# Weight pieces of the first stage converted in turn, and one attention half moved to earlier iterations

## The chip, the core and the metric

The kernel runs on one core of a Trainium2 chip. The metric is the time of one execution on the device in microseconds (us), as the median of several runs. The engines are TensorE (PE in the profile; its weight loads are PEld), VectorE (DVE), ScalarE (ACT), GpSimd (POOL) and SyncE (SP), which issues most DMA transfers. Each engine takes its instructions strictly in its own order. An instruction waits until what it needs is there, and all that stands behind it on that engine waits with it.

## What is computed

```python
p_packed = sm_attn(p, k, v)          # 8 batches, 8 heads, 576 keys, 32 packed rows, 64 wide
out = sm_attn(q, p_packed, p_packed) # second attention, over the 32 packed rows
x = out.transpose(0, 2, 1, 3).reshape(4608, 512)
h = x @ w_in                         # 512 x 2048, arrives as 64-bit floats
x = (h - tanh(h)) @ w_out            # 2048 x 512, arrives as 64-bit floats
# then a layer of 8 experts: every token goes to the expert of its largest gate
```

## The kernel before

**Stages.** The first stage computes the packed rows, the first attention, for 12 of 16 *units* (a unit is four heads of one batch); the other four units are done later. It also converts 24 of 32 weight pieces. The second stage goes over 16 half batches: each time 16 steps of a first layer (`up`, with tanh) and a second layer (`down`). The third stage runs the experts. Only the first stage is changed.

**One iteration `u` of the first stage** (14 of them) does for different units at once: k of unit u+1 is transposed on PE (`k_up`, line 318) and copied out by ACT (line 321, tile `kT`, one buffer); the exponential of unit u runs on ACT (`expo_b`, line 340); the weights of unit u-1 are turned (`e_up`: on DVE at line 351 for the units up to 7, on PE at line 358 with copies on ACT, line 362, and DVE, line 360, from unit 8 on); unit u-2 is multiplied with v on PE (`pack`, lines 371 and 373) and copied out by ACT (line 374, from a single buffer `po`); then the scores of unit u+1 are taken on PE (line 330), and DVE reduces them to a maximum (`expo`, line 334, tile `mx`).

**Weight pieces.** `plan` is the list of pieces, each 128 x 512 numbers of 64 bits: 16 of `w_in`, 16 of `w_out`. Piece i is loaded by SP (lines 202 and 170) into one of five buffers, when the piece that had it has been read; it is narrowed to 32 bits by ACT (line 125), POOL (line 126) and two passes on DVE (lines 131 and 133). That is all for `w_in`. A piece of `w_out` is then also split into a rounded part (ACT, line 184) and a rest (DVE, line 188), at the start of the next iteration ("late"). POOL writes a piece of `w_out` in place, so it comes after ACT; and its buffer is free only after line 133, that of `w_in` after line 131. Iteration u converts pieces 2u and 2u+1.

**Jobs.** The table `jobs` says which piece of side work an iteration appends after `expo`: `make_z` turns packed rows (DVE, line 216); `att_q`, `att_s`, `att_f`, `att_x`, `att_n`, `att_t`, `att_l` are the steps of the second attention for the first half of batch 0 (`att_s` on PE; `att_x` on DVE, lines 249 and 250, then ACT, line 252; `att_t` ends in `a_hi`, `att_l` in `a_lo` on DVE, line 270); `fuse` multiplies the packed rows with a quarter of `w_in` on PE (line 277), and `fuse_h` (ACT, line 281) and `fuse_l` (DVE, line 285) split this product into `wf_hi` and `wf_lo`. The first `up` of the second stage (lines 603 to 605) needs `a_hi`, `a_lo`, `wf_hi` and `wf_lo`; the first `down` (lines 629 to 631) accumulates in four banks, one of which was `po`.

Inside a stage each engine keeps the order of the code. Between the end of the first stage and the start of the second, the order on an engine is decided when the kernel is built, by what is expected to be ready first.

```python
for u in range(LA):                              # LA = 14, UA = 12
    ...                                          # share, k_up, e_up, expo_b
    for n in late: part_h(n)                     # w_out pieces of the iteration before
    for n in late: part_l(n)
    ...                                          # ACT and POOL part of the next pieces
    if 1 < u < UA + 2: pack(u - 2)
    if u + 1 < UA: score(u + 1); expo(u + 1)
    ...                                          # loads of k, v, pieces, p, q
    for fn in jobs.get(u, ()): fn()
    for x in range(done, due(u)): convert(x)     # pieces 2u, 2u+1
```

Of the kernel before, what the change touches and what calls it, by code (L numbers as in the profile page):

```python
# [27 lines left out]
NF = DFF // 128  # L28
# [10 lines left out]
HF = NF // 2  # L39
# [11 lines left out]
def attention_moe_kernel(ctx: ExitStack, tc: tile.TileContext, q, k, v, p, w_in, w_out, w_gate, w_og, w1, w2, out):  # L51
# [130 lines left out]
    def part_h(f):  # L182
        sv, hi, _ = part_of(f)
        act.activation(hi, sv, AF.Copy)
# [23 lines left out]
    def make_z(b, hs=range(4)):  # L208
        if b not in z_t:
            z_t[b] = ef.tile([128, 4, 32], F32, name="zt", bufs=2)  # L210
        z = z_t[b]
        for g in range(2):
            for h in hs:
                for e in range(2):
                    r = 64 * (h % 2) + 32 * e
                    vec.transpose(z[r:r + 32, 2 * g + h // 2], pp[32 * h:32 * h + 32, 2 * b + g, 32 * e:32 * e + 32])
# [3 lines left out]
    def load_q(b, hf, js=range(4)):  # L220
        if (b, hf) not in q_t:
            q_t[b, hf] = tmp["new"]("qt", [128, 4, HB, 32])
        qt = q_t[b, hf]
        src = q[b].rearrange("(j g) (i f s) d -> g f i j s d", g=2, f=2, s=HB)
        for j in js:
            for x in range(4):
                g, e = divmod(x, 2)
                sp.dma_start(qt[32 * x:32 * x + 32, j], src[g, hf, :, j, :, 32 * e:32 * e + 32])

    def att_q(b, hf):  # L230
        qT = tmp["qT"] = tmp["new"]("qT", [128, 4, HB, 32])
        vec.transpose(qT, q_t.pop((b, hf)))

    def att_s(b, hf):
        tmp["s2"] = tmp["two"]()
        for j in range(4):
            for g in range(2):
                r = slice(64 * g, 64 * g + 64)
                pe.matmul(tmp["s2"][g][32 * j:32 * j + 32, :HN], lhsT=z_t[b][r, j], rhs=tmp["qT"][r, j], start=True, stop=True)  # L239

    def att_f(b, hf):
        sT = tmp["sT"] = tmp["new"]("sT", [128, TB, NP])
        for g in range(2):
            vec.transpose(sT[:, HB * g:HB * g + HB], tmp["s2"][g][:, :HN].rearrange("p (t i) -> p t i", i=32))

    def att_x(b, hf):
        sT = tmp["sT"]
        mx = tmp["new"]("amx", [128, TB, 1])
        vec.tensor_reduce(mx[:, :, 0], sT, axis=AX.X, op=ALU.max)
        vec.tensor_tensor(sT, sT, mx.to_broadcast([128, TB, NP]), op=ALU.subtract)  # L250
        ex = tmp["ex"] = tmp["new"]("ex", [128, TB, NP])
        act.activation(ex, sT, AF.Exp, scale=0.125)

    def att_n(b, hf):
        ex = tmp["ex"]
        sm = tmp["new"]("asm", [128, TB, 1])
        vec.tensor_reduce(sm[:, :, 0], ex, axis=AX.X, op=ALU.add)
        vec.tensor_scalar(sm, sm, 1e-9, None, op0=ALU.add)
        vec.reciprocal(sm, sm)
        tmp["mul"].tensor_tensor(ex, ex, sm.to_broadcast([128, TB, NP]), op=ALU.mult)  # L260

    def att_t(b, hf):
        aT = tmp["aT"] = tmp["new"]("aT", [128, TB, 32])
        vec.transpose(aT, tmp["ex"])
        a_hi[b, hf] = ap_.tile([128, 2, HN], F32R, name="a_hi")
        act.activation(a_hi[b, hf].rearrange("p g n -> p (g n)"), aT.rearrange("p t i -> p (t i)"), AF.Copy)

    def att_l(b, hf):
        a_lo[b, hf] = ap_.tile([128, 2, HN], F32R, name="a_lo")
        vec.tensor_tensor(a_lo[b, hf].rearrange("p g n -> p (g n)"), tmp["aT"].rearrange("p t i -> p (t i)"), a_hi[b, hf].rearrange("p g n -> p (g n)"), op=ALU.subtract)  # L270

    def fuse(b, n):
        tmp["pw"] = tmp["two"]()
        for j in range(4):
            for g in range(2):
                r = slice(64 * g, 64 * g + 64)
                pe.matmul(tmp["pw"][g][32 * j:32 * j + 32], lhsT=z_t[b][r, j], rhs=w_in_sb[r, j, 512 * n:512 * n + 512], start=True, stop=True)  # L277

    def fuse_h(b, n):
        for g in range(2):  # L280
            act.activation(wf_hi[n][:, g], tmp["pw"][g], AF.Copy)

    def fuse_l(b, n):
        for g in range(2):
            vec.tensor_tensor(wf_lo[n][:, g], tmp["pw"][g], wf_hi[n][:, g], op=ALU.subtract)  # L285
# [26 lines left out]
    def k_up(u, c):  # L312
        if c == 0:
            kT_t[u] = get["unit"]("kT").rearrange("p (t h i) -> p t h i", h=4, i=32)
        pk = get["unit"]("pk")
        for t in range(3):
            x = 6 * c + 2 * t
            pe.transpose(pk[:, 128 * t:128 * t + 128], k_t[u][:, x:x + 2].rearrange("p s d -> p (s d)"), ident)  # L318
        kT = kT_t[u].rearrange("p t h i -> p t (h i)")
        kT = kT[:, 3 * c:3 * c + 3] if u < BY_TURN else kT.rearrange("p (g t) n -> p t g n", t=3)[:, c]  # L320
        act.activation(kT, pk[:, :384].rearrange("p (t n) -> p t n", t=3), AF.Copy)
# [20 lines left out]
    def share(u):  # L342
        rs = rs_t[u]
        vec.tensor_scalar(rs, rs, 1e-9, None, op0=ALU.add)
        vec.reciprocal(rs, rs)
# [28 lines left out]
        act.activation(pp[:, u], po[:, :D], AF.Copy, scale=rs)  # L374


    plan = [(load_w_in, conv_in, n) for n in range(16)] + [(load_w_out, conv_out, n) for n in range(NF)]
    ahead = [0]

    def load_ahead(done):  # L380
# [8 lines left out]
    with ExitStack() as pa:  # L389
# [66 lines left out]
        def make_p(c):  # L456
            pk = ps_k.tile([128, 4, 128], F32, name="pk")
            for n in range(4):
                pe.transpose(pk[:, n], pr[c % 2][:, n].rearrange("p a d -> p (a d)"), ident)
            act.activation(pT[:, 4 * c:4 * c + 4], pk, AF.Copy, scale=0.125)  # L460
            for n in range(4 * c, 4 * c + 4):
                pT_t[n] = pT[:, n]
# [39 lines left out]
        for a in range(4):  # L502
            r = slice(32 * a, 32 * a + 32)
            pool.tensor_copy(foldm[r], ident[r, r].rearrange("p (o c) -> p o c", o=1).to_broadcast([32, 4, 32]))
        jobs = {4: [lambda: make_z(0, (0,)), lambda: make_z(0, (1,))], 5: [lambda: make_z(0, (2,))], 6: [lambda: att_q(0, 0), lambda: make_z(0, (3,))],
                7: [lambda: att_s(0, 0)], 8: [lambda: att_f(0, 0), lambda: make_z(1, (0,))], 9: [lambda: att_x(0, 0)],
                10: [lambda: att_n(0, 0), lambda: make_z(1, (1,))], 11: [lambda: att_t(0, 0), lambda: make_z(1, (2,))],
                12: [lambda: att_l(0, 0), lambda: fuse(0, 0)], 13: [lambda: fuse_h(0, 0), lambda: fuse_l(0, 0), lambda: make_z(1, (3,))]}
        late, done = [], 0
        LA = UA + 2  # L510
        def due(u):
# [5 lines left out]
        for u in range(LA):  # L517
            if u + 1 < UA and (u + 1) % 4 == 0:
                make_p((u + 1) // 4)
            if 0 < u <= UA:  # L520
                share(u - 1)
            if u + 1 < UA:
                k_up(u + 1, 0)
                k_up(u + 1, 1)
            if 0 < u <= BY_TURN:
                e_up(u - 1)
            if u + 1 < UA:
                k_up(u + 1, 2)
            if BY_TURN < u <= UA:
                e_up(u - 1)  # L530
            if u < UA:
                expo_b(u)
            for n in late:
                part_h(n)
            for n in late:
                part_l(n)
            if u < UA:
                for i in range(done, due(u + 1)):
                    fold_next(i)
            if u == UA:  # L540
                fold_next(NA)
            if 1 < u < UA + 2:
                pack(u - 2)
            if u + 1 < UA:
                score(u + 1)
                expo(u + 1)
            if 0 < u and u + 3 < UA:
                load_k(u + 3)
            if 1 < u < UA:
                load_v(u)  # L550
            load_ahead(done)
            if u in (1, 5) and 4 * (2 + u // 4) < UA:
                load_p(2 + u // 4)
            if 1 < u < 6:
                load_q(0, 0, [u - 2])
            if u % 4 == 2 and u < UA - 4:
                dup_p(u // 4 + 1)
            if u == 4:
                load_gates()
            for fn in jobs.get(u, ()):  # L560
                fn()
            if u == 7:
                vec.tensor_copy(wgt[:, :, 0:2 * NE], wgr)
            late = []
            want = due(u)
            for x, (_, conv, n) in enumerate(plan[done:want]):
                convert(done + x)
                if conv is conv_out:
                    late.append(n)
            done = want  # L570
# [4 lines left out]
    with ExitStack() as pb:  # L575
# [258 lines left out]
        for i, (b, hf) in enumerate(halves):  # L834
            n = b + 1
# [34 lines left out]
            if i in MOVED:  # L870
                u = UA + MOVED.index(i)
# [398 lines left out]
```

## Time and profile before

| | us |
|---|---|
| median of 3 runs | 1255.59 (1254.53 to 1258.48) |
| profiled execution, its own time | 1254.63 |
| span in the trace of that execution | 1252.9 |
| PE busy | 1190.7 (95%) |
| DVE busy | 885.6 (71%) |
| ACT busy | 560.9 (45%) |
| POOL busy | 454.8 (36%) |
| first `up` of the second stage | at 113.02 |
| first `down` of the second stage | at 117.47 |

The times are of one execution. The span is the distance from the first to the last instruction; the 1.7 us between it and the execution's own time lie around it. A time "at" is counted from the start of the span. PE's share is an average over stages of different kinds: the first stage takes less than a tenth of the span.

### The profile page before, as it was taken

How to read it: one execution, taken by the hardware profiler on the slowest of the kernel's cores; microseconds unless marked ns; L12 is line 12 of the kernel's file. 1: busy time of each engine (PE TensorE's matmuls, PEld its weight loads, DVE VectorE, ACT ScalarE, POOL GpSimd, SP SyncE). 2: the span in 40 equal slices, each digit the busy share in tenths (PEclk: the TensorE clock that was granted, in tenths of full speed). 3: DMA queues.
4: the chain of work that ended last, by engine and by line, in shares of the span. 5: the costliest groups of instructions: out<-in, count | busy, mean ns of one | idle time of the engine just before them, and what ended most of it. 6: DMA issues, size and time to landing. Idle time of an engine off the chain costs nothing.

```text
span 1252.9 us, 28221 instructions
## 1 busy us (share of the span) xinstructions
PE 1190.7 (95%) x10676; PEld 1107.7 (88%) x10676; DVE 885.6 (71%) x2045; ACT 560.9 (45%) x1264; POOL 454.8 (36%) x754
## 2 busy tenths in 40 slices
PE   6766999999999999999999999999999999999996
PEld 4545798998989989989989989899999999999996
DVE  4577967867777777777678667865677776777771
ACT  4454544434444434443443443543444554445541
POOL 5533303412421431341243134217335533454343
PEclk9787999999999999999999999999999999999998
DMA  9984420220220310211201001517666766677641
GB/s 346 297 237 106 107 58 20 39 60 20 48 58 16 76 33 17 32 38 18 42 20 33 8 20 54 99 61 188 201 201 214 225 218 200 200 221 228 203 143 39
DMA packets 133620, 139.19 MB, mean 111 GB/s; under 512 B 93507, under 2 KB 96579, under 8 KB 133475
## 3 DMA queue, kind: packets, MB, share of 16 engines
q1 hardware_dynamic: 122515, 118.21, 34.0%
q0 software_dynamic: 10960, 19.10, 5.1%
q8 instruction: 85, 1.39, 0.5%
q14 instruction: 60, 0.49, 0.2%
HBM read 118.20 MB, written 19.04 MB: 110 GB/s over the span
## 4 chain that ended last, share of the span: by engine, by line
PE 56%; issue 19%; POOL 15%; DVE 6%; DMA 2%; ACT 1%; POOLq 0%; SPq 0%; ACTq 0%; DVEq 0%
POOL out_dram L1049 12%; PE acc L630 10%; PE acc L631 10%; PE acc L629 10%; PE ph L603 6%; PE ph L605 5%; PE ph L604 5%; PE px L277 3%; PE po L371 1%; DMA kt<-in_k_dram 1%; DMA cvw<-in_moe_w_in_dram 1%; POOL gap L716 1%; PE pk L318 1%; PE px L646 1%; PE px L239 1%
## 5 line engine op out<-in xcount | busy, mean ns | idle before, releaser
L1049 POOL DMA_INDIRECT out_dram<-y,iqs x135 | 156.5, 1160 | 196.9 <-DVE y L1046 166.1
L711 POOL DMA_INDIRECT tab<-tok,ix x48 | 54.8, 1141 | 423.2 <-DVE ix L709 416.2
L617 DVE TENSOR_TENSOR gl<-gg,gh 128x288 fp32r<-128x288 f32 x256 | 115.5, 451 | 84.0 <-ACT gh L616 82.3
L616 ACT ACTIVATE gh<-gg 128x288 fp32r<-128x288 f32 x256 | 112.9, 441 | 131.7 <-PE acc L631 109.4
L603 PE MATMUL ph<-a_hi,wf_hi 128*128 128x288 f32 x512 | 161.7, 316 | 3.5 <-DVE wf_lo L285 2.8
L750 POOL DMA_INDIRECT xs<-x2s,ixr x144 | 145.2, 1008 | 49.4 <-issue 29.1
L609 DVE TENSOR_TENSOR gg<-ph,th 128x288 f32<-128x288 f32 x256 | 116.3, 454 | 62.0 <-ACT th L607 61.1
L607 ACT ACTIVATE th<-ph 128x288 f32<-128x288 f32 x256 | 104.6, 409 | 111.9 <-PE ph L605 110.3
L605 PE MATMUL ph<-a_hi,wf_lo 128*128 128x288 f32 x512 | 152.3, 297 | 1.6 <-DVE wf_lo L285 1.5
L1024 PE MATMUL ph<-xl,w1h 128*128 128x288 f32 x512 | 151.7, 296 | 1.8 <-DVE xl L1008 1.6
L630 PE MATMUL acc<-gl,wo_bt 128*128 128x288 f32 x512 | 151.7, 296 | 1.3 <-DVE gl L617 1.0
L630 PE MATMUL acc<-gl,wo_a 128*128 128x288 f32 x512 | 151.0, 295 | 1.3 <-DVE gl L617 1.3
L1023 PE MATMUL ph<-xh,w1h 128*128 128x288 f32 x512 | 151.4, 296 | 0.7 <-ACT xh L1007 0.5
L604 PE MATMUL ph<-a_lo,wf_hi 128*128 128x288 f32 x512 | 152.0, 297 | 0.0
L1041 PE MATMUL acc<-hh,w2l 128*128 128x288 f32 x512 | 151.6, 296 | 0.0
L1039 PE MATMUL acc<-hh,w2h 128*128 128x288 f32 x512 | 151.6, 296 | 0.0
L1040 PE MATMUL acc<-hl,w2h 128*128 128x288 f32 x512 | 151.5, 296 | 0.0
L629 PE MATMUL acc<-gh,wo_a 128*128 128x288 f32 x512 | 150.9, 295 | 0.5 <-ACT gh L616 0.5
L629 PE MATMUL acc<-gh,wo_bt 128*128 128x288 f32 x512 | 151.0, 295 | 0.3 <-ACT gh L616 0.3
L1025 PE MATMUL ph<-xh,w1l 128*128 128x288 f32 x512 | 150.9, 295 | 0.0
L631 PE MATMUL acc<-gh,wo_bt 128*128 128x288 f32 x512 | 150.7, 294 | 0.0
L631 PE MATMUL acc<-gh,wo_a 128*128 128x288 f32 x512 | 150.7, 294 | 0.0
(246 smaller groups left out, 2913.4 us busy)
## 6 DMA issues: line engine op xcount, KB each, us to landing
sraw<-in_moe_w_dram SPq DMA_DIRECT2D x64, 512.0 KB
raws<-in_moe_w_dram SPq DMA_DIRECT2D x56, 512.0 KB
xg<-xs SPq DMA_DIRECT2D x64, 144.0 KB
qt<-in_q_dram SPq DMA_DIRECT2D x240, 36.0 KB
kt<-in_k_dram SPq DMA_DIRECT2D x12, 576.0 KB
cvw<-in_moe_w_out_dram SPq DMA_DIRECT2D x13, 512.0 KB
cvw<-in_moe_w_in_dram SPq DMA_DIRECT2D x10, 512.0 KB
vt<-in_v_dram SPq DMA_DIRECT2D x8, 576.0 KB
```

The costliest lines, as they stand in the source:

```text
L603: pe.matmul(ph, lhsT=wf_hi[n][:, g, c], rhs=ah[:, g], start=g == 0, stop=False)
L604: pe.matmul(ph, lhsT=wf_hi[n][:, g, c], rhs=al[:, g], start=False, stop=False)
L605: pe.matmul(ph, lhsT=wf_lo[n][:, g, c], rhs=ah[:, g], start=False, stop=g == 1)
L629: pe.matmul(acc[j], lhsT=hi[:, j], rhs=gh, start=f == 0, stop=False)
L630: pe.matmul(acc[j], lhsT=hi[:, j], rhs=gl, start=False, stop=False)
L631: pe.matmul(acc[j], lhsT=lo[:, j], rhs=gh, start=False, stop=f == NF - 1)
L1023: pe.matmul(ph, lhsT=w1h[:, c, r], rhs=xh[:, c], start=c == 0, stop=False)
L1024: pe.matmul(ph, lhsT=w1h[:, c, r], rhs=xl[:, c], start=False, stop=False)
L1039: pe.matmul(acc[j], lhsT=w2h[:, f, j], rhs=hh, start=f == 0, stop=False)
L1040: pe.matmul(acc[j], lhsT=w2h[:, f, j], rhs=hl, start=False, stop=False)
L1041: pe.matmul(acc[j], lhsT=w2l[:, f, j], rhs=hh, start=False, stop=f == NF2 - 1)
L1049: apart("out", lambda: pool.indirect_dma_start(rows, bass.IndirectOffsetOnAxis(ap=iq[:, t:t + 1].bitcast(U32), axis=0), y[:, t], None, bou ...
```

## The change

`plan` has pieces of `w_in` and `w_out` in turn for its first 16 places, then the rest of `w_in`; before, all of `w_in` stood first. The first 24 places hold the same pieces as before. The jobs are in earlier iterations, and q is loaded one iteration sooner.

```diff
-    plan = [(load_w_in, conv_in, n) for n in range(16)] + [(load_w_out, conv_out, n) for n in range(NF)]
+    plan = [x for n in range(HF) for x in ((load_w_in, conv_in, n), (load_w_out, conv_out, n))]
+    plan += [(load_w_in, conv_in, n) for n in range(HF, 16)] + [(load_w_out, conv_out, n) for n in range(HF, NF)]
...
-        jobs = {4: [lambda: make_z(0, (0,)), lambda: make_z(0, (1,))], 5: [lambda: make_z(0, (2,))], 6: [lambda: att_q(0, 0), lambda: make_z(0, (3,))],
-                7: [lambda: att_s(0, 0)], 8: [lambda: att_f(0, 0), lambda: make_z(1, (0,))], 9: [lambda: att_x(0, 0)],
-                10: [lambda: att_n(0, 0), lambda: make_z(1, (1,))], 11: [lambda: att_t(0, 0), lambda: make_z(1, (2,))],
-                12: [lambda: att_l(0, 0), lambda: fuse(0, 0)], 13: [lambda: fuse_h(0, 0), lambda: fuse_l(0, 0), lambda: make_z(1, (3,))]}
+        jobs = {4: [lambda: make_z(0, (0,)), lambda: make_z(0, (1,))], 5: [lambda: make_z(0, (2,)), lambda: make_z(0, (3,)), lambda: att_q(0, 0)],
+                6: [lambda: att_s(0, 0), lambda: make_z(1, (0,))], 7: [lambda: att_f(0, 0), lambda: fuse(0, 0)],
+                8: [lambda: fuse_h(0, 0), lambda: fuse_l(0, 0), lambda: att_x(0, 0)], 9: [lambda: att_n(0, 0), lambda: make_z(1, (1,))],
+                10: [lambda: att_t(0, 0), lambda: make_z(1, (2,))], 11: [lambda: att_l(0, 0), lambda: make_z(1, (3,))]}
...
-            if 1 < u < 6:
-                load_q(0, 0, [u - 2])
+            if 0 < u < 5:
+                load_q(0, 0, [u - 1])
```

On DVE, from the reduction of unit 9 (in iteration 8) to that of unit 10 (in iteration 9), there stands before:

```order
L334 TENSOR_REDUCE mx<-sc 128x1
L244 STREAM_TRANSPOSE scr<-sc 128x288 x2
L216 STREAM_TRANSPOSE zt<-pp 32x32 x4
L131 SCALAR_TENSOR_TENSOR cvw<-cvw 128x512
L133 SCALAR_TENSOR_TENSOR cvw<-cvw 128x512
L131 SCALAR_TENSOR_TENSOR cvw<-cvw 128x512
L133 SCALAR_TENSOR_TENSOR cvw<-cvw 128x512
L344 TENSOR_SCALAR rs<-rs 128x1
L345 RECIPROCAL rs<-rs 128x1
L360 COPY eT<-pk 96x384
L188 TENSOR_TENSOR wo_a<-cvw,wo_a 128x512 x2
L334 TENSOR_REDUCE mx<-sc 128x1
```

and now:

```order
L334 TENSOR_REDUCE mx<-sc 128x1
L285 TENSOR_TENSOR wf_lo_107<-sc,wf_hi_106 128x512 x2
L249 TENSOR_REDUCE amx_a<-scr 128x18
L250 TENSOR_TENSOR scr<-scr,amx_a 128x576
L131 SCALAR_TENSOR_TENSOR w_in_sb<-cvw,w_in_sb 128x512
L133 SCALAR_TENSOR_TENSOR w_in_sb<-cvw,w_in_sb 128x512
L131 SCALAR_TENSOR_TENSOR w_in_sb<-cvw,w_in_sb 128x512
L133 SCALAR_TENSOR_TENSOR w_in_sb<-cvw,w_in_sb 128x512
L344 TENSOR_SCALAR rs<-rs 128x1
L345 RECIPROCAL rs<-rs 128x1
L360 COPY eT<-pk 96x384
L334 TENSOR_REDUCE mx<-sc 128x1
```

The product's lower part and `att_x` have moved in, `att_f` and one `make_z` have moved out, and the pair of line 188 is gone.

On ACT, from the copy-out of unit 6 (line 374) to the exponential of unit 9 (line 340), there stands before:

```order
L374 ACTIVATE pp<-po,rs 128x64
L321 ACTIVATE kT<-pk 128x3x128 x3
L362 ACTIVATE eT<-pk 96x384
L340 ACTIVATE e_sb,rs<-sc,mx 128x576
L184 ACTIVATE wo_a<-cvw 128x512 x2
```

and now:

```order
L374 ACTIVATE pp<-po,rs 128x64
L281 ACTIVATE wf_hi_106<-sc 128x512 x2
L252 ACTIVATE scr<-scr 128x576
L321 ACTIVATE kT<-pk 128x3x128 x3
L362 ACTIVATE eT<-pk 96x384
L340 ACTIVATE e_sb,rs<-sc,mx 128x576
```

The exponential of `att_x` (line 252) stands now ahead of the three copies of k of unit 10 (line 321), and the copies of line 184 behind them are gone.

On PE, from the scores of unit 11 (line 330) to the start of the second stage, there stands before:

```order
L330 MATMUL sc<-kT,scr 32x288 x8
L358 MATMUL pk<-ident,scr 96x128 x6
L373 MATMUL po<-vt,eT 32x64 x24
L358 MATMUL pk<-ident,e_sb 96x128 x6
L373 MATMUL po<-vt,eT 32x64 x24
L277 MATMUL sc<-w_in_sb,zt 32x512 x8
L373 MATMUL po<-vt,eT 32x64 x24
L603 MATMUL ph<-a_hi,wf_hi_106 128x288
```

and now, with the 18 matmuls of the first three `up` shortened to the first and the last:

```order
L330 MATMUL sc<-kT,scr 32x288 x8
L358 MATMUL pk<-ident,scr 96x128 x6
L373 MATMUL po<-vt,eT 32x64 x24
L358 MATMUL pk<-ident,e_sb 96x128 x6
L604 MATMUL ph<-a_hi,wf_hi_106 128x288
...
L606 MATMUL ph<-a_hi,wf_lo_107 128x288
L373 MATMUL po<-vt,eT 32x64 x48
L630 MATMUL acc_1720<-gh,wo_a 128x288
```

The product (line 277) has left this place, and three `up` of the second stage stand ahead of the `pack` of units 10 and 11. (The order counts a matmul of 32-bit floats once, the trace twice. Behind line 376 the changed kernel's line numbers are one higher.)

## Rows read from the trace of the kernel before

**Rows 1.** Page, part 2: 40 equal slices of 31.3 us; tenths.

```profile
PEclk9787999999999999999999999999999999999998
DMA  9984420220220310211201001517666766677641
```

**Rows 2.** Stretches: busy PE, PEld, DVE, ACT, POOL; then PEclk, DMA share, GB/s.

```profile
80.00:90.00 10.00, 6.20 (x184) 4.66 (x182) 9.65 (x20) 5.97 (x13) 2.87 (x2) 0.99 0.68 196
...
110.00:115.00 5.00, 2.18 (x16) 2.02 (x9) 2.11 (x6) 1.46 (x4) 1.19 (x1) 0.50 0.51 78
```

**Rows 3.** Who waited for whom, first 100 us (SPq: first 130 us): total, times, longest.

```profile
DVE mx L334 <- PE sc L330: 35.4, 8, 9.2
...
SPq L202 <- DVE w_in_sb L131: 12.3, 5, 4.3
```

**Rows 4.** Timeline of PE around 70 us: start, duration, operation, count, idle before.

```profile
67.87 0.47 PE L330 MATMUL sc<-kT,scr 64*32 64x288 f32 x7 [1.70 <-issue]
...
70.13 1.42 PE L371 MATMUL po<-vt,eT 32*32 32x64 f32 x87
...
76.87 1.75 PE L371 MATMUL po<-vt,eT 32*32 32x64 f32 x57 [5.31 <-issue]
```

**Rows 5.** Timeline of DVE, iterations 8 to 12.

```profile
79.88 0.76 DVE L334 TENSOR_REDUCE mx<-sc 128x1 f32<-128x576 f32 x1 [6.60 <-PE sc L330]
80.55 0.84 DVE L244 STREAM_TRANSPOSE scr<-sc 128x288 f32<-128x288 f32 x2
...
87.54 0.74 DVE L249 TENSOR_REDUCE amx_a<-scr 128x18 f32<-128x576 f32 x1
...
88.99 1.13 DVE L131 SCALAR_TENSOR_TENSOR st<-st 128x512 int32<-128x512 int32 x1
...
94.86 0.74 DVE L257 TENSOR_REDUCE asm_a<-scr 128x18 f32<-128x576 f32 x1
...
97.17 0.86 DVE L216 STREAM_TRANSPOSE zt<-pp 32x32 f32<-32x32 f32 x4
...
100.80 0.15 DVE L344 TENSOR_SCALAR rs<-rs 128x1 f32<-128x1 f32 x1
...
101.51 1.28 DVE L188 TENSOR_TENSOR wo_a<-cvw,wo_a 128x512 fp32r<-128x512 f32 x2
102.71 0.77 DVE L264 STREAM_TRANSPOSE scr<-scr 128x576 f32<-128x576 f32 x1
...
109.04 0.75 DVE L270 TENSOR_TENSOR a_lo<-scr,a_hi 128x576 fp32r<-128x576 f32 x1
...
111.58 1.29 DVE L285 TENSOR_TENSOR wf_lo<-sc,wf_hi 128x512 fp32r<-128x512 f32 x2 [1.79 <-ACT wf_hi L281]
```

**Rows 6.** Timeline of ACT and PE, the work between two reductions.

```profile
80.60 1.26 ACT L321 ACTIVATE kT<-pk 128x384 f32<-128x384 f32 x3 [1.62 <-PE pk L318]
...
81.99 2.21 PE L371 MATMUL po<-vt,eT 32*32 32x64 f32 x144
...
84.13 0.72 PE L330 MATMUL sc<-kT,scr 64*32 64x288 f32 x16
...
89.10 0.68 ACT L252 ACTIVATE scr<-scr 128x576 f32<-128x576 f32 x1 [1.26 <-DVE scr L250]
```

**Rows 7.** Timeline from the last `pack` into the second stage, all engines.

```profile
104.58 1.96 PE L277 MATMUL sc<-w_in_sb,zt 64*32 64x512 f32 x16
...
108.68 1.51 PE L373 MATMUL po<-vt,eT 96*32 96x64 f32 x48 [2.15 <-ACT pp L374]
...
110.26 0.31 ACT L374 ACTIVATE pp<-po,rs 128x64 f32<-128x64 f32 x1 [1.63 <-PE po L373]
...
113.02 0.58 PE L603 MATMUL ph<-a_hi,wf_hi 128*128 128x288 f32 x1 [2.82 <-DVE wf_lo L285]
...
117.47 0.44 PE L629 MATMUL acc<-gh,wo_a 128*128 128x288 f32 x1
...
118.59 0.68 DVE L131 SCALAR_TENSOR_TENSOR cvw<-cvw 128x512 int32<-128x512 int32 x1
```

## The prediction

> **What bounds the kernel now.** I read the page's slices first, then the stretches of the first stage, the list of waits, and last the timelines. The slices show that only the first four of 40 are the first stage; after them PE is granted its full clock and is the engine that counts, so what the first stage saves is kept by all that follows, and it can save nothing else [rows 1]. The stretches cut this stage in two. Up to about 78 us the DMA engines are nearly full (9, 9 and 8 tenths in the first slices). From 80 to 90 us DVE is busy 9.65 of 10 us while the share of DMA falls to 0.68 [rows 1, 2]. In the first part DVE has slack: its reduction waited 35.4 us in eight waits for the scores of PE [rows 3]. PE's largest pause is in the middle of a `pack`: 87 matmuls, then 5.31 us for nothing that the profile shows, then the other 57 [rows 4]. After it come the scores of unit 9, whose reduction on DVE starts at 79.88 after 6.60 us of idleness [rows 5]. From there to the start of the second stage DVE has no pause worth the name, so its queue is the path.
>
> At the end of the stage eT of unit 11 leads to the last `pack` at 108.68 (1.51), its copy-out at 110.26 (0.31), the upper and lower part of the product (1.29 on DVE) and the first `up` at 113.02; the first `down` follows at 117.47 [rows 5, 7]. I compare that `down`, since the changed order swaps what lies just before it.
>
> **The change, part by part.** First what DVE has to do from 79.88 on in the changed order, each length taken from start to start. A `make_z` and a pair of pieces take 3.63 (97.17 to 100.80), of which 0.86 is the `make_z`, so 2.77 the pair; shares and copy of eT 0.71 (100.80 to 101.51); a reduction 0.67 (79.88 to 80.55); `att_x` 1.45 (87.54 to 88.99); `att_n` 2.31 (94.86 to 97.17); `att_t` 0.77, `att_l` 0.75 and the product's lower part 1.29 (busy times) [rows 5].
>
> Iteration 8: 0.67 + 1.29 + 1.45 + 2.77 = 6.18, to 86.06. Iteration 9: 0.71, to 86.77, then the reduction of unit 10. This one has a **new wait**. The exponential of `att_x` stands on ACT ahead of the copies of k of unit 10. It can start when `att_x` is through on DVE, at 83.29, and takes 0.68; the copies take 1.26, to 85.23; behind them come the `pack` of unit 7 (2.21) and the scores (0.72) [rows 6], so that the reduction starts at about 88.2 and DVE has lost 1.4. In the kernel before those copies ran at 80.60 [rows 6]. Then 0.67 + 2.31 + 3.63 = 6.61, to 94.8. Iteration 10: 0.71 + 0.67 + 0.77 + 3.63 = 5.78, to 100.6. Iteration 11: 0.71 + 0.75, to 102.05, when `a_lo` is there. The scores and k of these iterations have time to be ready.
>
> The three `up` start then. In the trace it is 5.57 from the first of them (113.02) to the DVE pass that stands behind their third subtraction (118.59) [rows 7], so that DVE takes the last piece of `w_in` at 107.6; the piece 1.39 and the last eT 0.71 lead to 109.7, the last `pack` and its copy-out (1.51 + 0.31) to 111.5. There the bank of `po` is free and the first `down` starts: **6.0 earlier** than 117.47. `a_lo` so early is of little use by itself: what stands at the end is still the last `pack`.
>
> Against this, what moves ahead of 79.88. Seven or eight rests of `w_out` (1.20 for two from 101.51 to 102.71, so 0.60 each), `att_f` (0.84) and a `make_z` (0.86) come into iterations 1 to 8 [rows 5]; `att_q` and a `make_z` go from iteration 6 to 5, the q loads (DMA and SP) one iteration up past loads of k, v and pieces. The pieces of `w_out` give back their buffer one pass later (half a piece, 0.69), which holds up the loads behind it on SP. ACT's rounding of `w_out` stands ahead of the next copies. I take all this at nothing, because DVE's 35.4 us of waiting [rows 3] and PE's pause cover it and the number of bytes to load is the same; if there were no cover, DVE's part alone would be 8 x 0.60 + 0.84 + 0.86 = 6.5. The product itself (1.96 at half clock [rows 7]) goes to iteration 7, behind `att_f`, ahead of the 87 matmuls; between 71.5 and 76.87 PE stands still anyway, and it must only be over by then.
>
> One thing is not covered. From the end of the pause before, at 67.87, to this one there are 126 matmuls (14 of the scores, 16 of `att_s`, 9 of k, 87 of the `pack`), each with its weight load, so about 252 instructions [rows 4]. The pause seems to go with the number of instructions, as if the next block of them came late behind the loads. With the product's 16 ahead of it, it comes some 17 matmuls sooner in the `pack`, and 74 instead of 57 are left after it, at 1.75 / 57 = 0.031 each: 0.5 later [rows 4]. The sum is 6.0 - 0.5 = **5.5 us less**. The bounds of what I set at nothing are -2 (q out of the way of iteration 5's loads) and +3.
>
> The Trainium skill (Runtime: NRT & Kernel Launch, Instruction fetch mechanics) says that instructions are refilled in blocks of 256 and that a crossing is mostly hidden. The trace agrees with the 256, by my count, and not with the hidden cost, with 5.31 us in the row. By the page the pause would be another wait that stays at its matmul, and the sum would be 6.0, which is within the first case below.
>
> **The rivals.** *Half clock at the first `down`.* PE is granted half its clock (1.2 GHz) in parts of the stage: 0.50 in the stretch from 110 to 115 us, in which the 18 matmuls from 113.02 on run; their 4.45 are 0.25 each, and later slices show the clock full, 2.4 GHz [rows 1, 2, 7]. In the changed order the same 18 are followed by pauses of about 1.5 us and by two small `pack`. If the clock isn't full after that, the next 18 matmuls take 4.45 again instead of half, and the next product 1.96 instead of half: 2.2 + 1.0 = 3.2. That leaves 2.3 less: 1253.3. For it: pauses and small work; against: the same 18 matmuls come before.
>
> The Trainium skill (TensorE: Matmul & The Clock Gate, Part 1) says that the throttled clock is the default and that activity releases it. The trace agrees, with 0.50 in the stretch that begins with PE's pauses, and by that rule the pauses speak for this rival.
>
> *The cover in iterations 5 and 6 is thin.* `make_z`, `att_q` and two rests of `w_out` are new there; the reduction of unit 9 may come up to 3 later. 5.5 - 3 = 2.5 less: 1253.1.
>
> *The loads starve* (slower). An iteration ends with the pieces, and their buffers gate the next loads: SP waited 12.3 us in five waits on the first pass [rows 3]. If that loop, and not the amount of data, sets the pace up to 78 us, each of seven iterations is longer by a rest and a second pass, 0.60 + 0.69, with `att_f` and `make_z` 9.0 + 1.7 = 10.7 in all: 5.2 more than before, 1260.8. It decides from 5.5 on, half of that price. Against it: the DMA engines' 9, 9 and 8 tenths [rows 1], and DVE's waits.
>
> *The pause shrinks.* With q gone one iteration earlier, PE may get its instructions sooner; half of 5.31 more is saved: 1247.4.
>
> *It does not do what it says.* If the wait for the scores of unit 10 grows (the `pack` of unit 7 at half clock, and again in iterations 10 and 11), the DVE work saved is only waited for: up to 3 of the 6, 1253.
>
> **How the numbers follow.** The profiled execution took 1254.63, 0.96 under the median. 1254.63 - 5.5 = 1249.1, on the scale of the median 1250.1. Chances: the sum holds to about 2 us 0.53; half clock 0.15; thin cover or grown waits 0.15; pause shrinks 0.08; starved loads 0.09. The range leaves out most of the starved loads and the far end of the shrunk pause: 1246.5 to 1256. A measurement of this kernel can tell some 0.3%, 3.8 us, from no change, so faster means under 1251.8: most of the first case (0.48), the shrunk pause (0.08) and the lucky part of the two small cases (0.05), 0.61 in all; slower is most of the starved loads, 0.07; the rest is 0.32.
>
> **What would show it.** Right: the first `down` near 111.5 to 112; the reduction of unit 10 waiting for PE about 1.5 us; line 188 gone from DVE after 80 us; the reduction of unit 9 near 80.4, with PE's pause about 17 matmuls sooner in its `pack`; full clock at the first `down`. Wrong: a reduction of unit 9 beyond 83, the DMA share falling before 70 us, or the second stage's first `down` at half clock.

## The result

The changed kernel takes **1263.15 us** (median of 21 runs, 1256.15 to 1265.78), the kernel before beside it 1255.38 (21 runs, 1253.09 to 1259.43): a ratio of **1.0054** (95% interval 1.0045 to 1.0063), 6.8 us slower by the ratio (the medians are 7.8 apart). The prediction, 1250.1 with a range to 1256.0, was **wrong in size and in sign**.

| | before | changed |
|---|---|---|
| profiled execution, its span (us) | 1254.63, 1252.9 | 1262.89, 1261.2 |
| reduction of unit 9 (`mx`, line 334) starts | 79.88 | 85.56 |
| reduction of unit 11 starts | 94.18 | 104.68 |
| first `down` | 117.47 | 121.47 |
| first half-batch drained (`x2s<-acc`) | 164.47 | 170.25 |

Up to the drain 5.8 us are lost. The rest of the span is 1088.4 us before and 1091.0 after. The ten experiments below that ran on chips like the first had anything from 1085.6 to 1091.9 there, so I look for no cause in these 2.5 us.

The same views of the changed kernel as for before: the page's slices (tenths), stretches (busy PE, PEld, DVE, ACT, POOL; then PEclk, DMA share, GB/s), and waits (total, times, longest):

```profile
PEclk9866999999999999999999999999899999999998
DMA  9965330220220320210201001516666776677641
```

```profile
60.00:70.00 10.00, 4.10 (x59) 3.77 (x62) 7.74 (x18) 4.65 (x10) 3.74 (x3) 0.66 0.91 306
70.00:80.00 10.00, 5.42 (x146) 2.49 (x136) 4.38 (x9) 2.25 (x6) 5.96 (x4) 0.67 0.49 151
80.00:90.00 10.00, 6.59 (x178) 5.46 (x176) 6.45 (x12) 6.14 (x14) 3.07 (x2) 0.82 0.51 156
```

```profile
DVE mx L334 <- PE sc L330: 30.0, 7, 9.2
...
PE pk L460 <- POOL scr L466: 12.5, 2, 6.5
...
SPq L202 <- DVE w_in_sb L131: 12.7, 5, 5.6
```

Beside [rows 1 to 3]: PE's granted clock is 6 tenths in the third and in the fourth slice, in place of 8 and 7, DVE is no longer full from 80 to 90 us (6.45 for 9.65), and the DMA engines are idle half of the time there (0.51 for 0.68), so the amount of bytes is not the limit there. SP's waits for DVE ahead of the loads of pieces (lines 170 and 202, first 100 us) come to 34.5 us in all, before to 34.2. What has grown is a wait of PE for POOL, 12.5 us in two, at line 460: the transposes of p (`make_p`), which need POOL's copy of p (`dup_p`, line 466). No step of the prediction named it. The kernel before has one such wait (its lines are 459 and 465), and its second copy is in time:

```profile
PE pk L459 <- POOL scr L465: 3.8, 1, 3.8
```

```profile
55.79 0.84 DVE L216 STREAM_TRANSPOSE zt<-pp 32x32 f32<-32x32 f32 x4
...
57.89 0.78 POOL L465 COPY scr<-scr 128x256 f32<-128x256 f32 x1
...
60.67 0.66 PE L459 MATMUL pk<-ident,scr 128*128 128x128 f32 x4
```

**Where the copy got late.** The timelines of all engines in the changed kernel, first the first wait in one row, then what stands ahead of the second:

```profile
30.17 1.11 PE L460 MATMUL pk<-ident,scr 128*128 128x128 f32 x4 [6.05 <-POOL scr L466]
...
54.98 1.72 DVE L216 STREAM_TRANSPOSE zt<-pp 32x32 f32<-32x32 f32 x8
56.73 1.38 DVE L232 STREAM_TRANSPOSE scr<-scr 128x1152 f32<-128x1152 f32 x1
...
60.12 0.69 DVE L133 SCALAR_TENSOR_TENSOR cvw<-cvw 128x512 int32<-128x512 int32 x1
...
60.85 0.63 ACT L184 ACTIVATE wo_a<-cvw 128x512 fp32r<-128x512 f32 x1 [3.80 <-DVE cvw L133]
61.38 0.64 ACT L125 ACTIVATE cvw<-st 128x512 f32<-128x512 f32 x1
...
62.11 1.62 POOL L126 TENSOR_SCALAR st<-st 128x512 f32<-128x512 f32 x1 [4.88 <-ACT cvw L125]
63.70 1.50 POOL L126 TENSOR_SCALAR w_in_sb<-st 128x512 f32<-128x512 f32 x1
65.15 0.70 POOL L466 COPY scr<-scr 128x256 f32<-128x256 f32 x1
...
65.90 1.12 PE L460 MATMUL pk<-ident,scr 128*128 128x128 f32 x4 [6.47 <-POOL scr L466]
66.81 2.13 PE L318 MATMUL pk<-ident,kt 128*128 128x128 f32 x9
68.87 2.51 PE L371 MATMUL po<-vt,eT 32*32 32x64 f32 x129
74.28 0.64 PE L371 MATMUL po<-vt,eT 32*32 32x64 f32 x15 [2.90 <-issue]
```

Read it from 54.98 on. Iteration 5 now has two `make_z` (1.72; before one, 0.84) and `att_q` (1.38) ahead of its conversions. The last DVE pass over a `w_out` piece (L133) is so much later. ACT's `part_h` (L184) waits for it, and ACT's reads of the next pieces (L125) stand behind that. POOL's sign instruction for a `w_out` piece writes **in place** (`st<-st`; that for `w_in` writes into `w_in_sb`, which is free), so it waits for ACT's read. The copy of p stands behind it in POOL's queue, and all of PE behind the copy. PE's next work runs at half its clock: the granted clock is 0.50 from 65.9 to 69.0 us, where it was full (1.00) ahead of the wait, from 57.0 to 59.4. The pause for nothing that the profile shows, before one of 5.31 us inside the `pack` of iteration 8 [rows 4], is now one of 2.90 in iteration 7. The Trainium skill (PSUM — Partial Sum Buffer, Engine vs sequencer instructions) calls the queues of ScalarE, VectorE and GpSimdE strictly first in, first out; these rows agree: POOL's copy, whose p SP had asked for at 17.70, starts when the two instructions ahead of it are done. The first copy stands in a like chain: POOL's in-place instruction ahead of it, at 25.89, waits 1.83 for ACT's read. What made that wait longer than before isn't followed here.

**Where iteration 9 lost.** PE, ACT and DVE from the reduction of unit 9 to that of unit 10:

```profile
85.56 0.76 DVE L334 TENSOR_REDUCE mx<-sc 128x1 f32<-128x576 f32 x1 [1.25 <-PE sc L330]
...
89.00 0.68 ACT L252 ACTIVATE scr<-scr 128x576 f32<-128x576 f32 x1 [2.81 <-DVE scr L250]
89.59 1.24 ACT L321 ACTIVATE kT<-pk 128x384 f32<-128x384 f32 x3
...
90.12 1.28 PE L358 MATMUL pk<-ident,scr 128*96 128x128 f32 x6 [3.53 <-ACT kT L321]
...
91.33 3.37 PE L371 MATMUL po<-vt,eT 32*32 32x64 f32 x144
...
94.63 0.68 PE L330 MATMUL sc<-kT,scr 64*32 64x288 f32 x6
...
96.85 0.70 PE L330 MATMUL sc<-kT,scr 64*32 64x288 f32 x10 [1.53 <-issue]
...
97.61 0.76 DVE L334 TENSOR_REDUCE mx<-sc 128x1 f32<-128x576 f32 x1 [5.27 <-PE sc L330]
```

This is the wait that was predicted, 5.27 us in place of 1.4. The exp starts 3.44 after the reduction, as worked out (3.41). But the transposes of e (L358) also stand between the kT copies and the `pack` (1.2, left out of the sum), the `pack` runs at a granted clock of 0.62 after PE's wait (3.37 for the 2.21 that it takes at full clock), and a pause of 1.53 falls between the scores: 3.9 together.

### The profile page after: what moved, and what is told of

Its sections match the earlier page's. It is cut to its first block, busy times and chain, and to the rows that moved or that the text cites. A ratio compares the mean times of both kernels' runs of the same rounds, so it can differ in the third digit from the quotient of the medians.

```text
span 1261.2 us, 28200 instructions
## 1 busy us (share of the span) xinstructions
PE 1195.3 (95%) x10676; PEld 1114.1 (88%) x10676; DVE 886.6 (70%) x2045; ACT 560.1 (44%) x1264; POOL 455.2 (36%) x754
## 3 DMA queue, kind: packets, MB, share of 16 engines
HBM read 118.20 MB, written 19.04 MB: 109 GB/s over the span
## 4 chain that ended last, share of the span: by engine, by line
PE 55%; issue 18%; POOL 15%; DVE 6%; ACT 1%; POOLq 0%; DVEq 0%; ACTq 0%
POOL out_dram L1050 12%; PE acc L631 10%; PE acc L632 10%; PE acc L630 10%; PE ph L604 6%; PE ph L606 5%; PE ph L605 5%; PE px L277 3%; POOL gap L717 1%; PE px L647 1%; PE po L371 1%; PE px L239 1%; POOL xs L751 1%; DVE gl L618 1%; DVE gg L610 0%
## 5 line engine op out<-in xcount | busy, mean ns | idle before, releaser
L608 ACT ACTIVATE th<-ph 128x288 f32<-128x288 f32 x256 | 104.7, 409 | 115.8 <-PE ph L606 111.5
```

## Experiments

Theory at first: the copy of p is late because of the order of the pieces. Rival: the sooner jobs lose by themselves. Each time is given with its ratio to the kernel before, run beside it, and ratios are what is compared between groups. The first four runs:

```diff
-            if u % 4 == 2 and u < UA - 4:
-                dup_p(u // 4 + 1)
+            if u in (1, 5):              # ahead of this iteration's fold_next
+                dup_p(u // 4 + 1)
```

**Copy sooner**, both copies, in the changed kernel. 

> The changed kernel, with the copy of p on POOL (dup_p, line 466) one iteration sooner, ahead of that iteration's sign instructions. Theory (the copy stands on POOL behind in-place sign instructions of w_out pieces, which wait for ACT, and PE's transposes of p wait for the copy): PE's waits of 6.05 us at 30.17 and 6.47 us at 65.90 go, mx of unit 8 starts at 68 to 71 us instead of 76.2, the first down at 113 to 117 instead of 121.5, and the kernel takes 6 to 9 us less than the changed one: 1254 to 1257 us. Rival (the mixed order of the pieces itself holds the pass, by loads or by DVE, and PE would have waited for the copy's place in any case): mx of unit 8 stays at 74 us or later, 1260 us or more.

Measured 1254.39, ratio 0.9994 (0.9985 to 1.0003): some 8 us come back. PE waits for neither copy, and the reduction of unit 8 starts at 67.55, as the theory said or a little better:

```profile
25.11 0.66 PE L460 MATMUL pk<-ident,scr 128*128 128x128 f32 x4
...
59.26 1.11 PE L460 MATMUL pk<-ident,scr 128*128 128x128 f32 x4
```

Both copies count. Against the changed kernel the reduction of unit 4 comes 5.6 us sooner (31.79 for 37.34), by the first copy; 3.8 of this are left at unit 7, and at unit 8, behind the second, it is 8.6.

**Order alone** (`plan` of the changed kernel, `jobs` and `load_q` of before). 

> The kernel before, with the new order of the pieces alone (plan); jobs and loads of q as before. Theory (the order of the pieces makes the copy of p late): mx of unit 8 at 74 to 78 us instead of 68.7, the first down 5 to 9 us later than 117.5, 1260 to 1265 us. Rival (the sooner jobs hold the pass, because their DVE and PE work stands on the path): mx of unit 8 at 69 to 70 us, 1254 to 1257 us.

Measured 1254.62, 0.9989 (0.9977 to 1.0001), reduction of unit 8 at 69.08. **The theory fell**: the new order alone does not lose. The same chain of rows, without the work in iteration 5:

```profile
57.31 0.69 DVE L133 SCALAR_TENSOR_TENSOR cvw<-cvw 128x512 int32<-128x512 int32 x1
...
58.57 0.66 ACT L125 ACTIVATE cvw<-st 128x512 f32<-128x512 f32 x1
...
59.31 1.61 POOL L126 TENSOR_SCALAR st<-st 128x512 f32<-128x512 f32 x1 [3.11 <-ACT cvw L125]
...
62.35 0.40 POOL L466 COPY scr<-scr 128x256 f32<-128x256 f32 x1
...
62.80 0.66 PE L460 MATMUL pk<-ident,scr 128*128 128x128 f32 x4 [1.07 <-POOL scr L466]
```

The rows of DVE, ACT and POOL stand 2.80 or 2.81 sooner than in the changed kernel and PE's row 3.10; PE waits 1.07 for 6.47 (it also comes to this place 2.3 later). The order puts the copy behind the in-place work; the jobs make that work late. At the first copy PE still waits, 4.69.

**Jobs alone** (`plan` of before). 

> The changed kernel with the old order of the pieces (all of w_in first); jobs and loads of q as changed. Theory: the copy of p is in time as before (PE waits 4 us at about 28 and not at 60), mx of unit 9 starts at 79 to 82 us, the shorter DVE queue behind it brings the first down to 112 to 116 us, 1250 to 1254 us. Rival (exp of the second attention ahead of the kT copies on ACT, and the product on PE, cost as much as the shorter queue gives): mx of unit 10 starts 5 us after its scores could, first down at 117 us or later, 1255 to 1258 us.

Measured 1262.15, 1.0057 (1.0039 to 1.0074): as slow as the whole change, and both theories missed it. The copy of p was in time for the second transposes (58.38; no wait there), and still the reduction of unit 9 came at 83.10; the rival's own loss, the wait for the scores of unit 10, is there too (10.55 us from the reduction of unit 9 to it, before 6.99). So the jobs lose by themselves, and more than the rival allowed.

**Copy sooner in the kernel before.** 

> The kernel before, with the copy of p on POOL one iteration sooner, as in the first run. Theory: it takes away only the 3.80 us that PE waits for it at 28.5 us, and part of that is waited for elsewhere: mx of unit 8 at 65 to 69 us, 1252 to 1256 us. Rival (the copy is a bound of the pass in either order of the pieces): 1250 us or less.

Measured 1254.05, 0.9992 (0.9981 to 1.0004): without the change the place of the copy is worth little in time, though the drain came 3.6 sooner in its one trace.

A second theory followed: two separate losses, the copy and the exp ahead of the kT copies. The exp (line 252) is moved behind the exp of unit 9:

```diff
     def att_x(b, hf):          # its DVE part stays in jobs[8]
-        act.activation(ex, sT, AF.Exp, scale=0.125)
...
                 expo_b(u)
+            if u == 9:
+                att_e(0, 0)    # the exp
```

These kernels and four relatives first ran on two other chips, whose stages after the first take longer (kernel before: 1394.63 and 1402.62). So the next four were run beside each other on one like the first.

**The changed kernel again.** 

> The changed kernel itself, on the chip of the three runs below. Both theories: the first half-batch ends at 169 to 172 us, 6 to 8 us above the kernel before.

 Measured 1262.62, 1.0056 (1.0035 to 1.0077), drain at 169.21.

**Exp later, copy late.** 

> The changed kernel with the exp of the second attention later and the copy of p left late, on the chip of the changed kernel. Theory (the exp ahead of the kT copies costs 4 to 5 us by itself): 4 to 5 us below the run of the changed kernel. Rival (covered by other waits of the time, or given back later): within 2 us of it.

 Measured 1257.01, 1.0009 (0.9995 to 1.0022): 5.6 less, a little over the theory. On one of the other chips it had 0.9974 (0.9944 to 1.0004).

**Both.** 

> The changed kernel with both mends (copy of p sooner, exp later), on the same chip. Theory (the two losses are separate and add up, 9 for the copy and 4 for the exp): 12 to 14 us below the run of the changed kernel, 4 to 6 below the kernel before. Rival (they overlap): 9 to 10 us below the changed kernel.

 Measured **1249.87, 0.9943** (0.9921 to 0.9964): 12.75 below the changed kernel, and faster than before. On the other chips it had 0.9928 (0.9899 to 0.9956) and 0.9897 (0.9851 to 0.9943). The losses add up: 7.8 for the copies and 5.6 for the exp, each alone. Iteration 9 in this kernel:

```profile
77.20 0.76 DVE L338 TENSOR_REDUCE mx<-sc 128x1 f32<-128x576 f32 x1 [0.40 <-PE sc L334]
...
78.56 1.26 ACT L325 ACTIVATE kT<-pk 128x384 f32<-128x384 f32 x3
...
79.12 0.91 PE L362 MATMUL pk<-ident,scr 128*96 128x128 f32 x6 [0.89 <-ACT kT L325]
...
79.96 2.21 PE L375 MATMUL po<-vt,eT 32*32 32x64 f32 x144
...
81.49 0.68 ACT L256 ACTIVATE scr<-scr 128x576 f32<-128x576 f32 x1 [0.59 <-DVE scr L250]
...
84.75 0.74 DVE L338 TENSOR_REDUCE mx<-sc 128x1 f32<-128x576 f32 x1
...
107.65 0.40 PE L636 MATMUL acc<-gh,wo_a 128*128 128x288 f32 x1 [0.43 <-ACT pp L378]
...
154.65 1.65 DVE L646 STREAM_TRANSPOSE x2s<-acc 128x288 f32<-128x288 f32 x4
```

ACT's wait for DVE (0.59 for 2.81) is behind the kT copies now, the `pack` has its full clock (granted 1.00), and the reduction of unit 10 follows in 7.55 us, in place of 12.05. Other traces say the same: from the reduction of unit 9 to that of unit 11 pass 18.7 to 20.8 us in all six with the changed jobs and the exp where it was, and 14.1 to 15.5 in all six with the exp later and the product left where it was.

**Order and copy, old jobs.** 

> New order of the pieces and copy sooner with the old jobs, on the same chip. Theory (the sooner jobs, mended, gain 1 to 2 us in all, since what the tail wins is partly lost in iterations 5 and 7 to the work put there): 1 to 3 us above the run before. Rival (jobs are worth nothing at all): the same time or less.

 Measured 1250.17, 0.9952 (0.9934 to 0.9970). On the other chips it had 0.9930, where both mends had 0.9928, and 0.9945 (0.9921 to 0.9968), where they had 0.9897 (0.9851 to 0.9943). All three pairs lean towards the sooner jobs, none is clear of noise: **what the sooner jobs, mended, are worth by themselves is undecided**, and order and copy give the 6 us without them. (Alone, order has 0.9989 and copy 0.9992.)

**Work of iteration 5 behind its conversions**, in the changed kernel: `jobs[5]` is called after the loop over `convert`. 

> The changed kernel, with the jobs of iteration 5 (z of heads 2 and 3, transpose of q) on DVE behind that iteration's two conversions instead of ahead of them; nothing else. Theory (these 2.2 us of DVE delay the conversion that ACT's part_h of the w_out piece waits for, behind it ACT's reads, POOL's sign instructions and the copy of p, and so PE): the copy starts at 62 to 63.5 us instead of 65.2, PE waits 3 to 4.5 us for it instead of 6.5, 2 to 3 us below the changed kernel (1262.6 to 1263.2): 1259.5 to 1261 us. Rival (POOL's place is set by the loads or by ACT's other work): copy at 65 us, 1262 us or more.

Measured 1255.55, 1.0010 (0.9997 to 1.0022), against 1.0056 for the changed kernel: some 6 us (3 to 9 by the two intervals), more than the theory said. All of this trace is 3 us later up to the reduction of unit 6 (57.13 for 54.20), so the copy stands at 65.29 again; but from that reduction to the copy it is 8.16 in place of 10.95, the 2.8 that the theory named. PE's wait for the copy is 0.43; another 2.47 goes to `att_s`, which now waits for `att_q`:

```profile
64.35 1.22 PE L239 MATMUL sc<-scr,zt 64*32 64x288 f32 x16 [2.47 <-DVE rs L344]
66.00 1.12 PE L460 MATMUL pk<-ident,scr 128*128 128x128 f32 x4 [0.43 <-POOL scr L466]
```

**Both mends and this.** 

> Both mends (copy sooner, exp later) with the jobs of iteration 5 behind its conversions. Theory (once the copy is early nothing on PE waits for that chain): within 1 us of both mends alone (1249.87). Rival (the in-place chain holds the pass beside the copy, by the slots of the pieces): 1 to 3 us less, 1247 to 1249 us.

 Measured **1245.14, 0.9943** (0.9927 to 0.9958): the same ratio as both mends alone, as the theory said, but the intervals (some 2 to 3 us to either side) don't exclude the rival's 1 to 3 us. These two, and order and copy with the old jobs, beat both kernels.

On the other chips only: **jobs and copy, old order.** 

> Old order of the pieces (all w_in first), the sooner jobs and loads of q, and the copy of p one iteration sooner: the last but one of the eight combinations of order, jobs and copy. Theory (the late copy costs the jobs more than it costs the kernel before, because they leave PE nothing to do meanwhile): mx of unit 8 at 67 to 69 us, 1253 to 1257 us, 6 to 9 us less than jobs alone (1262.15). Rival (the copy matters only in the new order; jobs in the old order lose by themselves): 1259 to 1262 us.

 0.9976 (0.9946 to 1.0006), which fits the theory, with the reduction of unit 9 at 77.93; 3.9 us are won already at unit 4 (31.77 for 35.67 with jobs alone), by the first copy. **Product later**, with both mends, in iterations 9 and 10. 

> The run before, and the product of z and w_in in iteration 9 with its two halves in iteration 10, instead of 7 and 8. Theory (in iteration 7 the product waits 1.67 us for DVE and runs 1.96 us, both on PE's path): mx of unit 9 comes 2 to 3.5 us sooner, but 2 us of it go in iteration 9, 0 to 2 us less than the run before. Rival (PE waits for kT and DVE in iteration 8 all the same): same time within 1 us, or up to 2 us more since wf_lo now stands in DVE's queue ahead of unit 11.

 0.9915 (0.9884 to 0.9946) against 0.9928 without; the reduction of unit 9 came 2.95 sooner (73.88 for 76.83), and a pause of 3.57 inside the product took it back. **In iterations 10 and 11.** 

> The changed kernel with the copy sooner, the exp later, and the product of z and w_in in iteration 10, its halves in iteration 11, where PE waits 3 us for ACT's exp of unit 11 in any case. Theory: mx of unit 9 comes 2 us sooner than with the product in iteration 7 and nothing is lost in iteration 10, 1247 to 1250 us. Rival (wf_lo in iteration 11 delays DVE by the 1.3 us of its two instructions, and PE's clock at half takes the rest): same as the run with the exp later, within 1 us.

 0.9936 (0.9906 to 0.9966) against 0.9897 (0.9851 to 0.9943): undecided.

## Why the prediction was wrong

The three parts of the first half-batch, from each kernel's own trace. These are single executions: three traces of the kernel with both mends reach unit 9 at 75.42 to 77.20 and the drain at 153.02 to 157.06, three with order and copy at 75.14 to 77.25 and 157.49 to 164.12.

| us | before | changed | copy sooner | both mends | order alone | jobs alone |
|---|---|---|---|---|---|---|
| to the reduction of unit 9 | 79.88 | 85.56 | 76.75 | 77.20 | 78.83 | 83.10 |
| from there to that of unit 11 | 14.30 | 19.12 | 19.04 | 15.07 | 14.01 | 18.83 |
| from there to the drain | 70.29 | 65.57 | 65.43 | 62.38 | 69.06 | 68.67 |
| drain at | 164.47 | 170.25 | 161.22 | 154.65 | 161.90 | 170.60 |

- **"I take all this at nothing" (what moves ahead of 79.88): the step that failed.** It cost 5.7, beyond the bound of 3. The step looked at the queues of DVE and SP; it named ACT's rounding as standing ahead of "the next copies" and never asked what on POOL waits for ACT. POOL's sign instructions had no term, and neither had PE's transposes of p. The cover was real for DVE (DVE's wait on the reduction is still 30.0 us), but the wait that grew was PE's, from 3.8 to 12.5 us. Both copies together are worth 0.0062 of the time (1.0056 to 0.9994), 7.8 us; moving the work of iteration 5, which bears on the second copy alone, gives some 6. The loss needs late copies and sooner jobs together: unit 9 comes at 83.1 to 87.0 in the five traces with both and the jobs of iteration 5 ahead of its conversions, at 78.8 to 79.9 with late copies and old jobs, at 73.9 to 78.3 in all with sooner copies. Two of the prediction's three signs of being wrong were seen (unit 9 beyond 83, half clock at the first `down`).
- **New wait of 1.4: right place, mis-sized.** It measured 5.27, by the three terms above, and moving the exp gave 5.6 us. The first `down` is 10.0 later than the sum had it (121.47 for 111.5): 5.7 by the failed step, 3.9 by this one, 0.4 elsewhere.
- **DVE's shorter queue, 6.0 sooner: right where nothing else waits, with some luck.** From the reduction of unit 9 to the first `down` I had 31.6 with the wait, so 30.2 without it; with both mends it is 30.45 (77.20 to 107.65), in the changed kernel 35.91. Two errors cancel in it: `a_lo` is there 22.0 after that reduction with both mends, not 20.8, and what follows takes 8.4, not 9.5; PE's clock is full for part of it. The gain of the tail needs both edits: from unit 11 to the drain 4.7 are gained in the changed kernel, 1.6 with jobs alone, 1.2 with order alone.
- **The pause, +0.5: wrong in place and sign.** It stands one iteration sooner, behind 129 matmuls, and is 2.90 for 5.31. The Trainium skill's rule (Runtime: NRT & Kernel Launch, Instruction fetch mechanics: refills of 256 instructions, mostly hidden) has the count again, 129 matmuls with as many weight loads. The cost is hidden at some crossings and not at others: between this pause and the one of 1.53 stand 381 matmuls, three times 127, and the two crossings between, by this count inside the `pack` at 81.75 and that at 91.33, show no pause. That the pauses are refills is argued from the count; no run tests it.
- **Rivals.** *Half clock at the first `down`*: it came (0.61 and 0.44 a matmul at 121.47, granted clock 0.51, as against 0.40 and 0.30 with both mends), and from there to the drain the changed kernel takes 48.8, before and both mends 47.0: 1.8 of the 3.2 that I gave it. *Waits for scores grow*: came in iteration 9, larger; in iteration 10 the `pack` took 0.88, at full clock. *Starved loads*: its time, 1260.8, was the nearest, but not its mechanism: the share of DMA is 0.91 from 60 to 70 us and falls (0.49 from 70 to 80) only behind PE's wait, SP's waits for DVE are the same in all (34.5 for 34.2), and order alone, with the same passes and buffers, is not slower. *Thin cover in iterations 5 and 6*: the right iteration and jobs for the second copy, with DVE as the engine that would be late and not POOL behind it.

The rows of the half clock at the first `down`, in the changed kernel:

```profile
121.47 0.61 PE L630 MATMUL acc<-gh,wo_a 128*128 128x288 f32 x1 [0.43 <-ACT pp L374]
121.87 0.44 PE L631 MATMUL acc<-gl,wo_a 128*128 128x288 f32 x1
```

Left open: why jobs alone lose 3.2 us ahead of unit 9 although the second copy is in time there. The loss is there at unit 7 (64.36 for 60.86), and that the copies matter for them too is seen (77.93 with them sooner); its whole path is not.

## To carry to other kernels

When work moves on one engine, follow each instruction that it delays to the engine that waits for it, and on to what stands behind that wait there: here 2.2 us on DVE went by way of ACT and an in-place write on POOL to PE, and some 6 us came back when they stood behind the conversions. A small copy that the busiest engine needs belongs ahead of waiting work in its queue, and a new instruction whose input comes late belongs behind the copies that feed that engine. A wait of PE is not priced by its length: of the 12.5 us for the copies 7.8 came back in the time, while the exp's 3.53 gave 5.6, with the lower clock behind them.

## What was not expected of the hardware

A stall of PE can cost more than its length. Behind 3.53 us of waiting the `pack` took 3.37 for 2.21, at a granted clock of 0.62; ahead of the wait the clock was full. The pause behind it is no part of that price: with both mends one of 0.95 stands in the same scores. Behind 6.47 us the four transposes of p took 1.12 us (0.66 with the order alone). But with the copy sooner they took 1.11 without any wait for it, behind a pause of 2.35 for nothing that the profile shows, so the lower clock at this place (granted 0.63 there) does not need that wait. And the same program ran a tenth longer on two chips than on the others, with the first stage alike: both pages list 145 packets of instructions, but there PE waits, in the stages behind, for nothing that the profile shows, where on the chip of the first runs it does not. The groups of one line of the third stage (busy, mean ns of one, idle before), first with the copy sooner on the chip of the first runs, then with both mends on one of the two:

```profile
L1041 PE MATMUL acc<-hl,w2h 128*128 128x288 f32 x512 | 151.9, 297 | 0.0
```

```profile
L1047 PE MATMUL acc<-hl,w2h 128*128 128x288 f32 x512 | 152.3, 297 | 8.5 <-issue 8.5
```

What held its instructions there I can't tell.
